# Two interleaved attention and dense layers on one core: where the last 128 output columns of a group are transposed

## The chip, the cores and the metric

The kernel runs on one core of one Trainium2 chip. The metric is the device time of one execution in microseconds (us). Before the change it is 1353.05 us, the median of 3 runs (1352.7 to 1353.13).

## The reference, cut to what matters

There are 2048 rows of width 640. A layer is a linear attention block (32 heads of 20) followed by a dense block of width 1728, each behind a layer norm and each added to its input. There are two layers with the same weights.

```python
x = x + _A_ref(_layernorm(x), A_wqkv, A_wo)      # attention block
x = x + _B_ref(_layernorm(x), B_w1, B_b1, B_w2, B_b2)   # dense block
# _B_ref: h = x @ w1 + b1;  h = max(h, 0) ** 2;  out = h @ w2 + b2
```

The change lies in the dense block, in how the last 128 of the 640 output columns get back into rows.

## The kernel before

**Tiling.** The rows are 16 tiles of 128. In the dense block a group `g` is four tiles (512 rows), so a layer has groups 0 to 3. Every matmul is done in three passes, from a high and a low part of each operand (`split`), and the sums stay in PSUM, whose eight banks of 128x512 floats have names (`FB`): `h` for fc1's result, `a0` to `a3` and `as` for fc2's sums, `po0` and `po1` for side products.

**Steps.** A group has 14 steps `c`, one for each chunk of 128 of the 1728 inner columns. In step `c`, `fc1` (L1005) makes 15 matmuls into bank `h`, transposed: inner columns on the partitions, the 512 rows of the group along the free axis. `act` applies the bias and the ReLU on ScalarE (L1017, which empties bank `h`), then squares and splits on VectorE (L1018, L1019, L1020). `fc2` (L1055) of the step before runs on TensorE behind the fc1 of this one: `pend` holds it back by one step. So TensorE's order is fc1(c), fc2(c-1), fc1(c+1), fc2(c), and fc2 of step 13 of group g runs in step 0 of group g+1.

**fc2.** It adds to five banks in the order of `i`: for `i` = 0 to 3 the bank `a<i>` holds 128 rows by output columns 0 to 511 (DM = 512). For `i` = 4 (TG) the weights and the rows change sides, and bank `as` holds output columns 512 to 639 on the partitions by all 512 rows of the group. This fifth part, the strip, is transposed and has to be turned.

**The end of a group.** In its last step fc2 does the strip first. `strip_out` (L1063) copies bank `as` to SBUF on ScalarE; TensorE goes on with `i` = 0 to 3; then `strip_turn` (L1069) does four transposes of 128x128 on TensorE into bank `po0`. On VectorE, four `tile_add`s (L1080) add the banks `a0` to `a3` to the residual rows in the tile `x1` (one buffer), and `strip_add` (L1073) adds the turned strip from `po0` to their last 128 columns. `x2_store` (L1084) then issues four stores of 128x640 on SP's queue, to the next layer's input or to the output. In the last group of the last layer `fc2_last` does the same in another order.

**What else runs beside the steps.** The attention output of the next group is made beside the steps of this one. Each step has places: `"pre"`, then 0 to 4 (after each part `i` of fc2), `"pe"` and `"post"`. A table `events`, keyed by (group, step, place), lists functions that are called there in the order in which they were entered; a place is written here as (step, place). `side` enters those of a pair of tiles. Of these, the following matter here:

- `blocks_T` (L356) and `blocks_move` (L365): a transpose without TensorE. VectorE turns each 32x32 block of a tile in place, and ScalarE then moves the blocks to their partitions with 16 copies of 32x160, four for each `j`.
- `p_split` (L1223 on ScalarE, L1225 on VectorE) and `s_turns` (L1208, L1212, L1215) prepare the operands of a pair. In groups 1 and 2, `s_turns` has its places at (8,0) to (8,3) for the second pair.
- `Pair.p1` to `p7` are the pair's products. They use the banks `po0` and `po1` in turn, in the order p1 (9,0), p4 (9,1), p6 (9,2), p7 (9,3), p5 (9,4). `p1` is read out of its bank by ScalarE (`su`, L1283), and p6 writes the same bank next; the others are added by VectorE (L1276).
- `f_bias` (L632, L633), `b_load_pq` (L573) and `b_load_x` (L577) issue stores and loads on SP.

In group 3 of layer 0, `side_last` prepares the first tiles of the next layer instead, with `blocks_move` after steps 7, 8, 9, 10, 12 and 13 and `xT_split` (L127, L128) after steps 9 and 11. Group 3 of layer 1 has no such work.

**Queues and buffers.** Every engine takes its instructions in the order written. SP issues nearly all transfers, in order: the weights come by `load_ring` (L288) into a ring of six buffers as soon as fc1 or fc2 has freed one. Working tiles of 128x640 come from one pool of twelve buffers (`ftile`). `x1_load` (L1136, at step 12) fills `x1` for the end of the group and needs the stores of the group before to be done.

Of the kernel before, what the change touches and what calls it, by code (L numbers as in the profile page):

```python
# [8 lines left out]
F32 = mybir.dt.float32  # L9
R32 = mybir.dt.float32r  # L10
AF = mybir.ActivationFunctionType
ALU = mybir.AluOpType

P = 128
# [7 lines left out]
TG = 4  # L22
GT = TG * P
B32 = 32
NG = NT // TG
# [29 lines left out]
    )  # L55

OUT0 = (3, 5, 8, 10)
TURN0 = (  # L60
# [11 lines left out]
def kernel(  # L72
# [11 lines left out]
    nc = tc.nc  # L84
# [36 lines left out]
    def ftile(name):  # L121
        return tmp.tile([P, D], F32, tag="f", name=name, bufs=F_BUFS)
# [284 lines left out]
    def rows(t, ap):  # L407
        return ap[t * P : (t + 1) * P, :]
# [23 lines left out]
    for layer in range(N_LAYERS):  # L432
# [54 lines left out]
        def rtile():  # L487
            return ap.tile([P, D], F32, tag="r", name="r", bufs=3)
# [26 lines left out]
        if layer == 0:  # L515
# [28 lines left out]
            out=mask, in_=mask, compare_op=ALU.is_ge, fill=0.0, base=0,  # L544
# [3 lines left out]
            out=mask, in_=mask, compare_op=ALU.is_ge, fill=0.0, base=DH - 1,  # L548
# [116 lines left out]
        for t in range(NT):  # L665
# [13 lines left out]
            if first:  # L679
                fk, fq = Phi(rtile()), Phi(rtile())  # L680
                for nm, f, pss in (("k", fk, (bank(0), bank(1))), ("q", fq, (bank(2), bank(7)))):
                    w = wk(nm)
                    for c in range(DC):
                        for j in range(2):
                            s = slice(j * HD, (j + 1) * HD)
# [17 lines left out]
            g = list(range(DC)) if t > 0 else []  # L703
# [9 lines left out]
            f, fq = Phi(rtile()), None if is_late else Phi(rtile())  # L713
# [248 lines left out]
        for i in (2, 3):  # L962
# [18 lines left out]
        bp = sb.enter_context(  # L981
            tc.tile_pool(name=f"b_{layer}", bufs=1, side="right", reuse_waits="tile")
        )

        def fresh(nm):
            return bank(FB[nm])
# [49 lines left out]
        accs, x1s = {}, {}  # L1036

        def fc2_tile(g, c, h, i):

            u = wu.get(g, "w2", c)  # L1040
            wh, wl = u[:, :D], u[:, D:]
            first, last = c == 0, c == NF - 1
            if first:
                accs[g, i] = fresh(f"a{i}" if i < TG else "as")
            ps = accs[g, i]
            if i < TG:
                hh, hl = (h[:, j, i * P : (i + 1) * P] for j in range(2))
                a = [(hh, wl[:, :DM]), (hl, wh[:, :DM]), (hh, wh[:, :DM])]
            else:
                hh, hl = h[:, 0], h[:, 1]  # L1050
                a = [(wl[:, DM:], hh), (wh[:, DM:], hl), (wh[:, DM:], hh)]
            if last:
                a = [a[0], a[2]]
            for k, (l, r) in enumerate(a):
                nc.tensor.matmul(  # L1055
                    ps, l, r, start=first and k == 0, stop=last and k == len(a) - 1
                )

        strips = {}

        def strip_out(g):
            strips[g] = s = bp.tile([P, GT], F32, tag="s", name="strip", bufs=1)
            nc.scalar.activation(s, accs.pop((g, TG)), AF.Copy)  # L1063

        def strip_turn(g):
            ps = fresh("po0")
            s = strips[g]
            for i in range(TG):
                nc.tensor.transpose(ps[:, i * P : (i + 1) * P], s[:, i * P : (i + 1) * P], ident)  # L1069
            strips[g] = ps  # L1070

        def strip_add(g):
            nc.vector.tensor_tensor(  # L1073
                out=x1s[g][:, :, DM:], in0=strips.pop(g)[:, :GT].rearrange("p (i n) -> p i n", i=TG),
                in1=x1s[g][:, :, DM:], op=ALU.add,
            )

        def tile_add(g, i, s=slice(0, DM)):
            v = x1s[g][:, i, s]
            nc.vector.tensor_tensor(out=v, in0=accs[g, i][:, s], in1=v, op=ALU.add)  # L1080

        def x2_store(g, i):
            t = TG * g + i
            nc.sync.dma_start(rows(t, of) if last_layer else x2[t], x1s[g][:, i])  # L1084

        def fc2(g, c, h, after=lambda i: None):
            if c < NF - 1:
                for i in range(TG + 1):
                    fc2_tile(g, c, h, i)
                    after(i)  # L1090
            else:
                fc2_tile(g, c, h, TG)
                strip_out(g)
                after(0)
                for i in range(TG):
                    fc2_tile(g, c, h, i)
                    if i < TG - 1:
                        after(i + 1)
                strip_turn(g)
                after(TG)  # L1100
                for i in range(TG):
                    tile_add(g, i)
                strip_add(g)
                for i in range(TG):
                    x2_store(g, i)
            wu.used(g, "w2", c)

        def fc2_last(g, h, hl):
# [62 lines left out]
        def m_turns(m):  # L1171

            b1 = m_whole(m)
            yield
            b2 = m_whole(m + 2)
            lo, hi = slice(0, HD), slice(HD, D)
            for i, (out, x, y) in enumerate((
                (b1[:, lo], b1[:, hi], b1[:, lo]),
                (b1[:, hi], b2[:, hi], b1[:, hi]),
                (b2[:, hi], b2[:, hi], b1[:, lo]),  # L1180
                (b2[:, lo], b2[:, lo], b2[:, hi]),
            )):
                if i % 2 == 0:
                    yield
                nc.vector.tensor_tensor(out=out, in0=x, in1=y, op=ALU.subtract)
            yield
            for u, v in ((ta, b1), (tb, b2)):
                nc.scalar.activation(u[:, 0, m], v, AF.Copy)
            for u, v in ((ta, b1), (tb, b2)):
                yield  # L1190
                nc.vector.tensor_tensor(
                    out=u[:, 1, m], in0=v, in1=u[:, 0, m].bitcast(F32), op=ALU.subtract
                )
# [134 lines left out]
        def steps(at, f, *places):  # L1328

            it = []  # L1330

            def go():
                if not it:
                    it.append(f())
                next(it[0], None)

            for p in places:
                at(*p, go)
# [44 lines left out]
        def side(g, p, plan, at):  # L1383

            t0, t1 = TG * g + 2 * p, TG * g + 2 * p + 1
            m0, m1, turn, out, back = plan["moves0"], plan["moves1"], plan["turn"], plan["out"], plan["back"]
            for t, (s, pl) in ((t0, m0), (t1, m1)):
                if t != TG:
                    at(s - 4, "post", lambda t=t: b_load_pq(t))
                den, blk = plan.get(("den", t - t0), ((s - 2, "post"), (s - 1, 1)))  # L1390
                at(*den, lambda t=t: b_den(t))
                at(*blk, lambda t=t: b_blocks(t))
                for k in range(4):
                    at(s + (pl + k) // 5, (pl + k) % 5, lambda t=t, k=k: blocks_move(yzp[t], (k,)))
            steps(at, lambda: p_split(t0), (m0[0] + 1, 0), (m0[0] + 1, 2))
            steps(at, lambda: p_split(t1, 2), (m1[0] + 1, 0), (m1[0] + 1, 1))
            steps(at, lambda: s_turns(t0), *turn)
            first = min(out.values(), key=lambda v: (v[0], v[1]))
            at(first[0] - 3, "post", lambda: b_load_x(t0))
            at(first[0] - 3, "post", lambda: b_load_x(t1))  # L1400

            def begin():
                pairs[t0] = Pair(t0)

            at(*first, begin)
            for nm, pl in out.items():
                at(*pl, lambda nm=nm: getattr(pairs[t0], nm)())

            for t, (st, ap_, (s, pl), hi, lo, bi) in ((t1, back[0]), (t0, back[1])):
                at(*st, lambda t=t: ln_stats(("b", t), xr[t]))  # L1410
                at(*ap_, lambda t=t: norm(t))
                for k in range(4):
                    at(s + (pl + k) // 5, (pl + k) % 5, lambda t=t, k=k: blocks_move(yzx[t], (k,)))
                steps(at, lambda t=t: x_split(t), hi, lo)
                at(*bi, lambda t=t: f_bias(t))


        events = {}
        for g in range(NG - 1):
            for p in range(TG // 2):  # L1420

                def at(s, place, f, g=g):
                    n = max(g * NF + s, 0)
                    events.setdefault((*divmod(n, NF), place), []).append(f)

                if g > 0:
                    side(g + 1, p, OUTS[p], at)
            if g == 0:
                for i, b in enumerate(OUT0):
                    single(i, b, OUT0[i - 1] if i else 1, at)  # L1430

                for m in range(2):
                    steps(at, lambda m=m: m_turns(m), *TURN0[m])
# [39 lines left out]
        for g in range(NG):  # L1473
            for c in range(NF):
# [10 lines left out]
                if pend:  # L1485
                    fc2(*pend, after=lambda i: run(g, c, i))
                    wu.load_ring()
                else:
                    for i in range(TG + 1):
                        run(g, c, i)  # L1490
# [46 lines left out]
```

## Time and profile before

| | us |
|---|---|
| median of 3 runs | 1353.05 |
| the profiled execution | 1352.46 |
| its span, first to last instruction | 1350.5 |
| TensorE matmul busy (6817) | 1342.5 (99%) |
| TensorE weight load busy (6817) | 1160.9 (86%) |
| VectorE busy (1625) | 912.1 (68%) |
| ScalarE busy (1931) | 770.2 (57%) |
| GpSimd busy (174) | 122.6 (9%) |

The granted TensorE clock is 1.000 over the span. The DMA queue that carries the data (q1) takes 53.8% of the time of 16 engines.

How to read the rows that follow in the prediction. A timeline row has the start and the length in us, then engine (PE is TensorE, DVE VectorE, ACT ScalarE, SPq SyncE's queue), line of the kernel, operation, output <- input, shape, and how many equal instructions were merged; a bracket gives the idle time before it and what ended it. Start times count from the first instruction. A matmul's record is longer than the time to the next one, since they are pipelined: starts are compared, not lengths. A row of the grouped view has the count, the total busy time in us, the mean of one in ns, then the idle time before.

### The profile page before, as it was taken

How to read it: one execution, taken by the hardware profiler on the slowest of the kernel's cores; microseconds unless marked ns; L12 is line 12 of the kernel's file. 1: busy time of each engine (PE TensorE's matmuls, PEld its weight loads, DVE VectorE, ACT ScalarE, POOL GpSimd, SP SyncE). 2: the span in 40 equal slices, each digit the busy share in tenths (PEclk: the TensorE clock that was granted, in tenths of full speed). 3: DMA queues.
4: the chain of work that ended last, by engine and by line, in shares of the span. 5: the costliest groups of instructions: out<-in, count | busy, mean ns of one | idle time of the engine just before them, and what ended most of it. 6: DMA issues, size and time to landing. Idle time of an engine off the chain costs nothing.

```text
span 1350.5 us, 19013 instructions
## 1 busy us (share of the span) xinstructions
PE 1342.5 (99%) x6817; PEld 1160.9 (86%) x6817; DVE 912.1 (68%) x1625; ACT 770.2 (57%) x1931; POOL 122.6 (9%) x174
## 2 busy tenths in 40 slices
PE   9999999999999999999999999999999999999998
PEld 8888998988888888888888899988888888888887
DVE  7888757777777676643467676677778667775323
ACT  5888858566546447411447688495756446464110
POOL 2222210000000000000012232100000000000000
PEclk9999999999999999999999999999999999999999
DMA  6787834574665484387521115156546646654744
GB/s 205 254 296 271 282 92 169 195 280 141 212 242 167 159 297 167 116 326 297 185 98 41 58 40 156 40 205 253 172 160 235 212 148 224 234 168 139 287 126 157
DMA packets 85635, 253.44 MB, mean 188 GB/s; under 512 B 11030, under 2 KB 19606, under 8 KB 84902
## 3 DMA queue, kind: packets, MB, share of 16 engines
q1 hardware_dynamic: 85398, 252.04, 53.8%
q8 instruction: 54, 0.88, 0.3%
q14 instruction: 39, 0.32, 0.1%
q10 hardware_dynamic: 144, 0.20, 0.0%
HBM read 193.50 MB, written 56.03 MB: 185 GB/s over the span
## 4 chain that ended last, share of the span: by engine, by line
PE 92%; DVE 4%; ACT 3%; issue 1%; POOL 0%; DMA 0%; DVEq 0%; ACTq 0%; POOLq 0%
PE PS L379 34%; PE PS L1005 28%; PE PS L1055 28%; ACT z L365 2%; PE PS L852 1%; PE PS L865 1%; DVE bn L336 0%; PE PS L521 0%; DVE kq L128 0%; DVE e L482 0%; DVE xr L621 0%; DVE r L483 0%; DVE xTb L128 0%; DMA Mr<-Mc 0%; POOL rs L341 0%
## 5 line engine op out<-in xcount | busy, mean ns | idle before, releaser
L365 ACT ACTIVATE z<-y 32x160 f32<-32x160 f32 x1424 | 475.9, 334 | 75.7 <-DVE y L356 59.4
L1005 PE MATMUL PS<-xTb,u 128*128 128x512 f32 x1400 | 333.8, 390 | 1.0 <-DVE xTb L128 1.0
L1005 PEld LDWEIGHTS PS<-xTb,u 128*128 128x128 f32 x1400 | 261.7, 188 | 54.9 <-DVE xTb L128 1.5
L379 PE MATMUL PS<-kq,xT 128*128 128x320 f32 (+2 forms) x1635 | 294.0, 334 | 1.1 <-DVE kq L128 0.6
L379 PEld LDWEIGHTS PS<-kq,xT 128*128 128x128 f32 x1635 | 259.0, 188 | 28.9 <-DVE rl L483 1.0
L1055 PE MATMUL PS<-u,h 128*128 128x512 f32 x1120 | 276.8, 390 | 0.0
L1055 PEld LDWEIGHTS PS<-u,h 128*128 128x128 f32 x1120 | 208.6, 188 | 40.8
L1017 ACT ACTIVATE hr<-PS,b1sb 128x512 f32<-128x512 f32 x104 | 71.4, 686 | 295.7 <-PE PS L1005 295.0
L1018 DVE TENSOR_TENSOR hr<-hr 128x512 f32<-128x512 f32 x104 | 71.8, 691 | 218.3 <-ACT hr L1017 217.9
L379 PE MATMUL PS<-kh,xh 128*128 128x512 f32 x480 | 124.3, 393 | 0.0
L475 ACT ACTIVATE e<-PS 128x320 f32<-128x320 f32 (+4 forms) x128 | 53.6, 435 | 102.5 <-PE PS L379 99.0
L340 POOL TENSOR_SCALAR rs<-mv 128x1 f32<-128x1 f32 x64 | 28.0, 438 | 871.1 <-DVE mv L338 871.1
L379 PE MATMUL PS<-uM,pT 128*128 128x320 f32 x648 | 102.6, 309 | 0.7 <-DVE uM L881 0.7
L379 PEld LDWEIGHTS PS<-uM,pT 128*128 128x128 f32 x648 | 97.7, 188 | 3.1 <-DVE uM L881 1.2
L379 PEld LDWEIGHTS PS<-kh,xh 128*128 128x128 f32 x480 | 87.4, 188 | 15.0
L482 DVE TENSOR_SCALAR e<-e 128x320 f32<-128x320 f32 (+4 forms) x128 | 42.6, 333 | 79.6 <-ACT e L475 79.2
L1055 PE MATMUL PS<-h,u 128*128 128x512 f32 x280 | 79.0, 390 | 0.0
L1020 DVE TENSOR_TENSOR h<-hr,h 128x512 fp32r<-128x512 f32 x104 | 72.0, 692 | 3.6
L650 POOL TENSOR_TENSOR acc<-acc,r 128x640 f32<-128x640 f32 x30 | 53.8, 1792 | 199.1 <-DVE r L483 199.1
L1055 PEld LDWEIGHTS PS<-h,u 128*128 128x128 f32 x280 | 52.2, 188 | 10.8 <-DVE h L1031 0.4
L1005 PE MATMUL PS<-xTb,uw 128*128 128x512 f32 x240 | 57.1, 389 | 0.0
L483 DVE SCALAR_TENSOR_TENSOR r<-PS,e 128x512 f32<-128x512 f32 (+2 forms) x104 | 51.1, 492 | 5.8 <-ACT e L475 2.3
(119 smaller groups left out, 1337.6 us busy)
## 6 DMA issues: line engine op xcount, KB each, us to landing
u<-kept_w SPq DMA_DIRECT2D x184, 640.0 KB, 4.7
x<-x SPq DMA_DIRECT2D x48, 320.0 KB, 5.7
kept_w<-uprep SPq DMA_DIRECT2D x23, 640.0 KB, 4.7
pqt<-pq SPq DMA_DIRECT2D x32, 320.0 KB, 4.6
x<-xr SPq DMA_DIRECT2D x32, 320.0 KB, 3.9
st<-in_B_w_dram SPq DMA_DIRECT2D x22, 320.0 KB, 5.8
pq<-r SPq DMA_DIRECT2D x20, 320.0 KB
kept_kq<-kq SPq DMA_DIRECT2D x10, 640.0 KB, 6.8
```

What stands on the lines that cost most here:

```text
L340: nc.gpsimd.tensor_scalar(rs, mv[:, 1:2], LN_EPS, None, op0=ALU.add)
L365: nc.scalar.activation(zv[j * B32 : (j + 1) * B32, :, i, :], yv[i * B32 : (i + 1) * B32, :, j, :], AF.Copy)
L379: nc.tensor.matmul(ps, a, b, start=first and i == 0, stop=last and i == 2)
L475: nc.scalar.activation(self.e[:, a:b], ps, AF.Exp)
L482: nc.vector.tensor_scalar(e, e, 1.0, PHI_EPS, op0=ALU.min, op1=ALU.add)
L483: nc.vector.scalar_tensor_tensor(out=self.r[:, a:b], in0=ps, scalar=0.0, in1=e, op0=ALU.max, op1=ALU.add)
L650: nc.gpsimd.tensor_tensor(out=acc, in0=acc, in1=r, op=ALU.add)
L1005: nc.tensor.matmul(ps, a[:, d, :], bb[:, d, :], start=d == 0 and i == 0, stop=d == DC - 1 and i == len(seq) - 1,)
L1017: nc.scalar.activation(r, ps, AF.Relu, bias=b1sb[:, c : c + 1])
L1018: nc.vector.tensor_tensor(out=r, in0=r, in1=r, op=ALU.mult)
L1020: nc.vector.tensor_tensor(out=h[:, 1], in0=r, in1=h[:, 0].bitcast(F32), op=ALU.subtract)
L1055: nc.tensor.matmul(ps, l, r, start=first and k == 0, stop=last and k == len(a) - 1)
```

## The change

In groups 0 to 2 of each layer (`beside`), the strip is no longer turned by TensorE. `strip_blocks` has VectorE turn the 32x32 blocks straight out of bank `as` into an SBUF tile, after the four `tile_add`s and in the place where `strip_add` was. `strip_moves` has ScalarE bring the blocks to their partitions with 16 copies of 32x128, four at each of the places (8,0), (8,2), (8,4) and (9,0) of the next group, into a tile `sz` from the pool of twelve. `strip_end` at (9,2) adds the result on VectorE and issues the four stores. These are entered in `events` ahead of the side work, so they come first at their places. `strip_out` and `strip_turn` remain for group 3.

```diff
+STRIP = ((8, 0), (8, 2), (8, 4), (9, 0), (9, 2))
...
+        def strip_tile():
+            return bp.tile([P, GT], F32, tag="s", name="strip", bufs=1)
+
         def strip_out(g):
-            strips[g] = s = bp.tile([P, GT], F32, tag="s", name="strip", bufs=1)
+            strips[g] = s = strip_tile()
             nc.scalar.activation(s, accs.pop((g, TG)), AF.Copy)
+
+        def strip_blocks(g):
+            y = strip_tile()
+            nc.vector.transpose(out=y, in_=accs.pop((g, TG)))
+            strips[g] = [y]
+
+        def strip_moves(g, j):
+            if j == 0:
+                strips[g].append(ftile("sz"))
+            y, z = (
+                a[:, :GT].rearrange("p (t j q) -> p t j q", t=TG, q=B32) for a in strips[g]
+            )
+            for i in range(P // B32):
+                nc.scalar.activation(
+                    z[j * B32 : (j + 1) * B32, :, i, :], y[i * B32 : (i + 1) * B32, :, j, :], AF.Copy
+                )
+
+        def strip_end(g):
+            strips[g] = strips[g][1]
+            strip_add(g)
+            for i in range(TG):
+                x2_store(g, i)
...
             else:
+                beside = g < NG - 1
                 fc2_tile(g, c, h, TG)
-                strip_out(g)
+                if not beside:
+                    strip_out(g)
                 after(0)
                 for i in range(TG):
                     fc2_tile(g, c, h, i)
                     if i < TG - 1:
                         after(i + 1)
-                strip_turn(g)
+                if not beside:
+                    strip_turn(g)
                 after(TG)
                 for i in range(TG):
                     tile_add(g, i)
-                strip_add(g)
-                for i in range(TG):
-                    x2_store(g, i)
+                if beside:
+                    strip_blocks(g)
+                else:
+                    strip_add(g)
+                    for i in range(TG):
+                        x2_store(g, i)
...
         for g in range(NG - 1):
+            for k, p in enumerate(STRIP):
+                f = (lambda g=g, k=k: strip_moves(g, k)) if k < 4 else (lambda g=g: strip_end(g))
+                events.setdefault((g + 1, *p), []).append(f)
             for p in range(TG // 2):
```

## The prediction

> **What bounds the kernel now.** I read the page first: the span, and the chain of work that ended last.
>
> ```profile
> span 1350.5 us, 19013 instructions
> ...
> PE 92%; DVE 4%; ACT 3%; issue 1%; POOL 0%; DMA 0%; DVEq 0%; ACTq 0%; POOLq 0%
> PE PS L379 34%; PE PS L1005 28%; PE PS L1055 28%; ACT z L365 2%; PE PS L852 1%; PE PS L865 1%; DVE bn L336 0%; PE PS L521 0%; DVE kq L128 0%; DVE e L482 0%; DVE xr L621 0%; DVE r L483 0%; DVE xTb L128 0%; DMA Mr<-Mc 0%; POOL rs L341 0%
> ```
>
> TensorE carries 92% of the chain, and L1005 and L1055 (fc1 and fc2 of the dense block, where the change is) carry 28% each. So in this stage a microsecond taken from TensorE is a microsecond of time, as long as no other engine becomes late. Next I read the timeline of TensorE around one turn, that at the end of group 0 in layer 0, and around a step with no turn, for comparison.
>
> ```profile
> 369.89 0.60 PE L1069 MATMUL PS<-ident,strip 128*128 128x128 f32 x4
> 370.25 3.70 PE L1005 MATMUL PS<-xTb,u 128*128 128x512 f32 x15
> 373.78 2.89 PE L1055 MATMUL PS<-u,h 128*128 128x512 f32 x12
> 376.51 0.84 PE L1055 MATMUL PS<-h,u 128*128 128x512 f32 x3
> ```
>
> ```profile
> 432.82 3.56 PE L1005 MATMUL PS<-xTb,u 128*128 128x512 f32 x15
> 436.22 0.84 PE L1055 MATMUL PS<-u,h 128*128 128x512 f32 x3
> ```
>
> The first column is the start. The four transposes begin at 369.89 and fc1 at 370.25, so they hold the array for 0.36 us, not for the 0.60 of their records, which overlap. The 15 matmuls of fc1 behind them take 373.78 - 370.25 = 3.53 us; without a turn ahead they take 436.22 - 432.82 = 3.40. So one turn costs 0.36 + 0.13 = 0.49 us. The last turn that the change touches (layer 1, group 2) has the same 3.53:
>
> ```profile
> 1256.40 3.69 PE L1005 MATMUL PS<-xTb,u 128*128 128x512 f32 x15
> 1259.93 1.29 PE L1055 MATMUL PS<-u,h 128*128 128x512 f32 x5
> ```
>
> **What the change removes.** Of the 32 transposes of the next row, 24 go: six turns of four. I call them turn 0, 1 and 2 of a layer, after the group that ends.
>
> ```profile
> L1069 PE MATMUL PS<-ident,strip 128*128 128x128 f32 x32 | 4.8, 272 | 0.0
> ```
>
> Gross saving: 6 x 0.49 = 2.94 us. (The record of one lasts 272 ns. The Trainium skill, TensorE: Matmul & The Clock Gate, Part 4: PE-mode transpose, gives about 275 ns for one in a kernel, and VectorE: DVE Perf Modes, Rules for kernel authors, says to do 128x128 transposes on TensorE where a PSUM destination is fine, which speaks against this change. The record agrees with the figure; by it the sum would be 24 x 0.275 = 6.6 us, but the starts above are 0.36 us apart for four.) The ScalarE copy L1063 goes as well; ScalarE is not on the path there, so that is worth nothing.
>
> **What then comes late.** With the turn gone, fc2 of the next step reaches bank a0 0.49 us earlier, and a0 must first have been read by the first of the four tile_adds (L1080). Timelines of VectorE at turn 0 of layer 0, and of VectorE and TensorE at the same turn of layer 1:
>
> ```profile
> 372.87 2.48 DVE L1080 TENSOR_TENSOR x<-PS,x 128x512 f32<-128x512 f32 x4
> 375.26 0.68 DVE L1073 TENSOR_TENSOR x<-PS,x 128x512 f32<-128x512 f32 x1
> ```
>
> ```profile
> 1040.03 2.48 DVE L1080 TENSOR_TENSOR x<-PS,x 128x512 f32<-128x512 f32 x4
> ```
>
> ```profile
> 1040.95 1.30 PE L1055 MATMUL PS<-u,h 128*128 128x512 f32 x5
> ```
>
> One add lasts 0.68 (the L1073 row has its shape) and they start 0.60 apart. At turn 0 the first ends at 373.55. How soon TensorE goes on after VectorE is read at the start of this stage:
>
> ```profile
> 254.15 1.55 DVE L128 TENSOR_TENSOR xTb<-PS,xTb 128x640 fp32r<-128x640 f32 x2
> ```
>
> ```profile
> 255.76 7.08 PE L1005 MATMUL PS<-xTb,u 128*128 128x512 f32 x30 [0.49 <-DVE xTb L128]
> 262.67 0.62 PE L1055 MATMUL PS<-u,h 128*128 128x512 f32 x2
> ```
>
> VectorE ends at 255.70, TensorE starts at 255.76: 0.06 us. The 30 matmuls then take 6.91, against 2 x 3.40 = 6.80: a restart costs another 0.11. So at turn 0 fc2 would like to start at 373.78 - 0.49 = 373.29, may start at 373.55 + 0.06 = 373.61, waits 0.32 and loses 0.11 more: 0.06 of the 0.49 is left. In layer 1 it wants 1040.46, gets 1040.03 + 0.68 + 0.06 = 1040.77: 0.31 + 0.11, so 0.07 is left. Nothing in the change makes these adds earlier; VectorE's work ahead of them is untouched. The later adds (0.60 apart) keep ahead of the matmuls on a1 to a3 (0.68 apart).
>
> At turn 1 (end of group 1) and turn 2 the adds are early enough:
>
> ```profile
> 481.88 2.48 DVE L1080 TENSOR_TENSOR x<-PS,x 128x512 f32<-128x512 f32 x4
> ```
>
> ```profile
> 483.27 2.88 PE L1055 MATMUL PS<-u,h 128*128 128x512 f32 x12
> 485.99 0.84 PE L1055 MATMUL PS<-h,u 128*128 128x512 f32 x3
> 486.67 0.62 PE L1005 MATMUL PS<-xTb,u 128*128 128x512 f32 x2
> ```
>
> ```profile
> 485.30 0.69 ACT L1017 ACTIVATE hr<-PS,b1sb 128x512 f32<-128x512 f32 x1
> ```
>
> ```profile
> 1256.49 2.48 DVE L1080 TENSOR_TENSOR x<-PS,x 128x512 f32<-128x512 f32 x4
> ```
>
> Turn 1: allowed at 481.88 + 0.68 + 0.06 = 482.62, wanted at 482.78. Turn 2 of layer 1: allowed at 1257.23, wanted at 1259.44. Two steps on, fc1 needs bank h, which the ReLU L1017 must have read: wanted at 486.67 - 0.49 = 486.18, allowed at 485.30 + 0.69 + 0.06 = 486.05. That spare of 0.13 is the tightest place of all; if it is missed, the loss is the shortfall plus 0.11. I take turns 1 and 2 at the full 0.49.
>
> **What the change adds.** On VectorE, strip_add (L1073, 0.68) is replaced by a block transpose of 128x512 from PSUM, which the trace doesn't show. Nearest row:
>
> ```profile
> L356 DVE STREAM_TRANSPOSE y<-pqt 128x640 f32<-128x640 f32 x32 | 27.0, 844 | 1.0
> ```
>
> It is for 640 columns; 128 fewer should save about a fifth, so I take 0.70 us, with 1.24 (the longest 128x640 row, xh<-xt L128, below) as the upper end; a shorter one gains nothing. It now also holds bank "as", which TensorE wants last of the five: at turn 0 at 373.61 + 0.11 + 2.73 = 376.45. It starts at 375.26, so it may last 1.13 before it costs anything; at turn 1 it starts at 481.88 + 4 x 0.60 = 484.28, "as" is wanted at 485.99 - 0.49 = 485.50, so 1.16. At 0.70: nothing.
>
> ```profile
> L128 DVE TENSOR_TENSOR xh<-xt,xh 128x640 fp32r<-128x640 f32 x32 | 39.5, 1235 | 0.0
> ```
>
> On ScalarE there are 16 new copies of 32x128 a turn, four each at places (8,0), (8,2), (8,4), (9,0). They are like L365, with 128 for 160 elements a partition; rows for the bounds:
>
> ```profile
> L365 ACT ACTIVATE z<-y 32x160 f32<-32x160 f32 x1424 | 475.9, 334 | 75.7 <-DVE y L356 59.4
> ```
>
> ```profile
> L1063 ACT ACTIVATE strip<-PS 128x512 f32<-128x512 f32 x8 | 4.7, 593 | 4.6 <-PE PS L1055 4.6
> ```
>
> A little below 0.334, I take 0.31, and 0.32 with the gap to the next; the far end is 0.593, and shorter ones gain nothing. Steps 8 and 9 of group 1, ScalarE, and the product p6 on TensorE:
>
> ```profile
> 429.72 0.69 ACT L1017 ACTIVATE hr<-PS,b1sb 128x512 f32<-128x512 f32 x1
> 430.30 0.52 ACT L1223 ACTIVATE pT<-z 128x384 fp32r<-128x384 f32 x1
> 434.94 1.26 ACT L1212 ACTIVATE uS<-z 128x640 fp32r<-128x640 f32 x2 [4.12 <-DVE z L1208]
> 436.42 0.69 ACT L1017 ACTIVATE hr<-PS,b1sb 128x512 f32<-128x512 f32 x1 [0.23 <-PE PS L1005]
> 437.97 0.44 ACT L1283 ACTIVATE su<-PS 128x320 f32<-128x320 f32 x1 [0.86 <-PE PS L379]
> ```
>
> ```profile
> 440.48 1.04 PE L379 MATMUL PS<-uT,uS 128*128 128x320 f32 x6
> ```
>
> The first eight copies (2.56) fit in the idle 4.12 ahead of uS. The third four follow uS: 436.20 + 1.28 = 437.48; the ReLU then takes 0.58 to the next start (430.30 - 429.72), so 438.06; the last four end at 439.34; su at 439.78. p6 (440.48) reuses the bank that su reads: spare 440.48 - 439.78 - 0.06 = 0.64. So this is hidden, at a price of nothing. In group 3 of layer 0 twelve copies (3.84) go into an idle time of 3.33 ahead of the ReLU of step 9:
>
> ```profile
> 647.36 0.69 ACT L1017 ACTIVATE hr<-PS,b1sb 128x512 f32<-128x512 f32 x1 [3.33 <-PE PS L1005]
> ```
>
> It is 0.5 late. An fc2 of 3.40 lies between it and the next fc1, and it takes 0.69, so about 2.5 was spare.
>
> strip_add comes back at (9,2) on VectorE, from SBUF (0.69, as in the next row), behind p4's add and ahead of p6's. The four stores go from step 0 to behind it on SP:
>
> ```profile
> 438.40 0.69 DVE L1020 TENSOR_TENSOR h<-hr,h 128x512 fp32r<-128x512 f32 x1
> ```
>
> ```profile
> 436.41 7.73 SPq L288 DMA_DIRECT2D u<-kept_w  x2
> ```
>
> ```profile
> 375.97 2.01 SPq L1084 DMA_DIRECT2D x<-x  x4
> ```
>
> The ReLU of step 9 starts at 437.48 in place of 436.42, 1.06 late, so L1020 ends near 440.15; with p4's add (half as wide as an add of 0.68) and itself, strip_add ends near 441.3. The four issues take 2.01, to 443.3; the next weight load is the second of the first SP row, which ends at 436.41 + 7.73 = 444.14. No load is held. In group 3 the load behind them may be 2 us late, and with six buffers in the ring and two units a step it is for a use three steps (20 us) on. The x1 tile, a single buffer, is wanted again only at step 12.
>
> **Sum.** 4 x 0.49 + 0.06 + 0.07 = 2.09 us. Against the profiled execution's 1352.46 (span 1350.5 and 2 us around it): 1350.4. That run lies 0.59 below the median of 1353.05, so the forecast for a median is **1351.0**, 0.15% faster; a measurement of this kernel can tell about 0.2% (2.7 us) from no change.
>
> **Rivals.**
> - *All six turns pay in full* (the adds are not the limit at turn 0): 1353.05 - 2.94 = 1350.1, 0.22% faster. Against it: 373.55 is the end of an add that must come first. 12%.
> - *The transposes cost their records*: 24 x 0.272 = 6.5 us, 1346.5. The starts, 0.36 apart for four, speak against it. (The Trainium skill's 275 ns, in TensorE: Matmul & The Clock Gate, Part 4, gives much the same.) 2%.
> - *The transpose out of PSUM is slow and holds bank "as"*: at 1.24 it costs 0.11 + 0.11 at the two turns 0, 0.08 + 0.11 at the two turns 1: 0.8, so 1351.8; at 1.6 it takes all of the gain: 1353.2. For it: no transpose here reads PSUM; against it: adds with a PSUM operand (0.68) are as fast as the same width in SBUF (0.69). 12%.
> - *Slower: the copies hold up su*, and TensorE waits for its bank at p6 in groups 1 and 2 of both layers. It decides from 440.48 - 0.06 - (436.20 + 0.58 + 0.44) = 3.20 for eight copies, 0.40 each. At the far end, 0.60 with its gap, each place loses 1.60 + 0.11, together 6.8: 1353.05 - 2.1 + 6.8 = 1357.8. Against it: the longer copy L365 takes 0.334. 8%.
>
> **How the numbers follow.** Forecast 66% (its own range 1350.6 to 1351.5). Faster by over 0.2%: the first two rivals, 0.14. Slower: the last, 0.08. Within 0.2%: 0.78. The range goes from 1350.0 (all turns in full) to 1353.2 (the slow transpose) and leaves out a tenth.
>
> **What would show it.** Right: TensorE waits about 0.3 us for the first tile_add at the two turns 0 and nowhere else new; fc1 behind a turn takes 3.40; the new transpose lasts about 0.70, a copy about 0.31; su ends more than 0.06 ahead of p6. Wrong: a wait of TensorE at p6, at "as", or on bank h two steps behind turn 1.

## The result, and the profile after

The changed kernel takes 1351.01 us, the median of 22 runs (1350.32 to 1351.31); the kernel before takes 1352.89 (1352.39 to 1353.82, 22 runs). The ratio is 0.9985, with a 95% interval of 0.9979 to 0.9991. The forecast was 1351.0. The gain of 1.9 us is 0.14%. The interval leaves out 1, but the gain is below the 0.2% that was set as the bound of what a measurement can tell; where it comes from is read from the traces.

The page of the changed kernel: its span, and TensorE's busy time.

```profile
span 1348.6 us, 19071 instructions
## 1 busy us (share of the span) xinstructions
PE 1340.0 (99%) x6793; PEld 1157.7 (86%) x6793; DVE 914.9 (68%) x1631; ACT 796.9 (59%) x2021; POOL 122.6 (9%) x174
```

24 matmuls fewer (6817 to 6793), 2.5 us less of TensorE. ScalarE has 90 instructions more and works 27 us longer, and TensorE does not wait for it: the new work lies beside TensorE's. Next, TensorE and VectorE at turn 0 of layer 0 (line numbers are now 2 higher in fc1 and fc2, 28 in tile_add: L1007, L1057, L1108).

```profile
368.81 1.30 PE L1057 MATMUL PS<-u,h 128*128 128x512 f32 x5
369.94 3.56 PE L1007 MATMUL PS<-xTb,u 128*128 128x512 f32 x15
373.65 3.05 PE L1057 MATMUL PS<-u,h 128*128 128x512 f32 x12 [0.15 <-DVE x L1108]
376.55 0.62 PE L1057 MATMUL PS<-h,u 128*128 128x512 f32 x2
```

```profile
372.92 2.48 DVE L1108 TENSOR_TENSOR x<-PS,x 128x512 f32<-128x512 f32 x4
375.31 0.71 DVE L1073 STREAM_TRANSPOSE strip<-PS 128x512 f32<-128x512 f32 x1
```

The transposes are gone and fc1 follows fc2 at once. But fc2 does not start at 369.94 + 3.40 = 373.34: it waits until the first tile_add (372.92 + 0.68 = 373.60) has left bank a0, and starts at 373.65. By the starts that is a wait of 0.31; the bracket has 0.15, because it counts from the end of the last record of fc1, and records are longer than the distance between starts. The part on bank "as" begins at 376.55, against 376.51 before the change, and this execution is 0.05 later since its start-up. So the turn has given 0.01, which is next to nothing. At turn 1, for comparison:

```profile
479.43 3.56 PE L1007 MATMUL PS<-xTb,u 128*128 128x512 f32 x15
482.83 2.88 PE L1057 MATMUL PS<-u,h 128*128 128x512 f32 x12
485.55 0.84 PE L1057 MATMUL PS<-h,u 128*128 128x512 f32 x3
486.23 1.98 PE L1007 MATMUL PS<-xTb,u 128*128 128x512 f32 x8
```

There fc1 takes 3.40, as without a turn, and the fc1 after it starts at 486.23 in place of 486.67; with the 0.05 of start-up that is the whole 0.49. The list of waits of TensorE has one new row (the last; the two before it are old):

```profile
PE PS L381 <- DVE uM L883: 0.7, 2, 0.4
PE PS L381 <- DVE GT L515: 0.4, 1, 0.4
PE PS L1057 <- DVE x L1108: 0.3, 2, 0.2
```

It comes twice, at the two turns 0, and counts like the bracket. What each turn gives can be read for every kernel in one way: take the start of the same matmul in the trace of before and in that of the kernel, well ahead of a turn and well behind it, and see by how much the difference changes. Start-up, which differs by up to 0.8 us from one execution to the next, drops out.

| kernel | turn 0 | turn 1 | turn 2 | turn 0 | turn 1 | turn 2 |
|---|---|---|---|---|---|---|
| (us; minus is gained) | layer 0 | | | layer 1 | | |
| the change | -0.01 | -0.49 | -0.49 | -0.01 | -0.49 | -0.49 |
| e1_adds_first | -0.20 | -0.49 | -0.49 | -0.23 | -0.49 | -0.49 |
| e2_two_groups | 0.04 | -0.49 | -0.49 | 0.04 | -0.49 | -0.49 |
| e3_turns_kept | 0.02 | 0.01 | 0.01 | 0.01 | 0.01 | 0.01 |
| e4_adds_first_moves | -0.50 | -0.49 | -0.49 | -0.50 | -0.49 | -0.49 |
| e7_before_adds_first | -0.01 | 0.00 | 0.00 | -0.01 | 0.00 | 0.00 |

The rest of the side work, steps 8 and 9 of group 1 on ScalarE, then VectorE's and SP's part of it:

```profile
434.98 1.26 ACT L1246 ACTIVATE uS<-z 128x640 fp32r<-128x640 f32 x2 [1.52 <-DVE z L1242]
436.26 1.26 ACT L1083 ACTIVATE sz<-strip 32x128 f32<-32x128 f32 x4
437.55 0.69 ACT L1019 ACTIVATE hr<-PS,b1sb 128x512 f32<-128x512 f32 x1
438.27 1.27 ACT L1083 ACTIVATE sz<-strip 32x128 f32<-32x128 f32 x4
439.56 0.44 ACT L1317 ACTIVATE su<-PS 128x320 f32<-128x320 f32 x1
```

```profile
440.55 0.68 DVE L1101 TENSOR_TENSOR x<-sz,x 128x512 f32<-128x512 f32 x1
```

```profile
441.26 2.00 SPq L1112 DMA_DIRECT2D x<-x  x4
443.86 0.32 SPq L290 DMA_DIRECT2D u<-kept_w  x1
```

```profile
440.52 1.04 PE L381 MATMUL PS<-uT,uS 128*128 128x320 f32 x6
```

su is out of its bank at 440.00 and p6 starts at 440.52, with no wait; the stores are issued by 443.26, and the weight load behind them goes out at 443.86.

### The profile page after: what moved, and what is told of

Same layout as the page of the kernel before. It is cut to its first block, busy times and chain, and to the rows that moved or that the text cites. A ratio compares the mean times of both kernels' runs of the same rounds, so it can differ in the third digit from the quotient of the medians.

```text
span 1348.6 us, 19071 instructions
## 1 busy us (share of the span) xinstructions
PE 1340.0 (99%) x6793; PEld 1157.7 (86%) x6793; DVE 914.9 (68%) x1631; ACT 796.9 (59%) x2021; POOL 122.6 (9%) x174
## 4 chain that ended last, share of the span: by engine, by line
PE 89%; DVE 5%; ACT 3%; issue 1%; DMA 1%; POOL 0%; SPq 0%; DVEq 0%; ACTq 0%
PE PS L381 34%; PE PS L1057 27%; PE PS L1007 27%; ACT z L367 2%; PE PS L854 1%; PE PS L867 1%; DMA st<-in_A_wqkv_dram 0%; DVE bn L338 0%; DVE e L484 0%; DVE xr L623 0%; DVE r L485 0%; DVE xTb L130 0%; DMA Mr<-Mc 0%; POOL rs L343 0%; DVE y L358 0%
## 5 line engine op out<-in xcount | busy, mean ns | idle before, releaser
L1007 PE MATMUL PS<-xTb,u 128*128 128x512 f32 x1400 | 333.1, 389 | 1.0 <-DVE xTb L130 1.0
L1007 PEld LDWEIGHTS PS<-xTb,u 128*128 128x128 f32 x1400 | 262.0, 188 | 55.3 <-DVE xTb L130 1.5
L1057 PE MATMUL PS<-u,h 128*128 128x512 f32 x1120 | 277.1, 390 | 0.3 <-DVE x L1108 0.3
L1057 PEld LDWEIGHTS PS<-u,h 128*128 128x128 f32 x1120 | 208.4, 188 | 41.9 <-DVE x L1108 1.2
L1057 PE MATMUL PS<-h,u 128*128 128x512 f32 x280 | 79.0, 390 | 0.0
L1057 PEld LDWEIGHTS PS<-h,u 128*128 128x128 f32 x280 | 52.1, 188 | 10.8 <-DVE h L1033 0.4
L1007 PE MATMUL PS<-xTb,uw 128*128 128x512 f32 x240 | 57.0, 389 | 0.0
```

The source lines that it names most:

```text
L1007: nc.tensor.matmul(ps, a[:, d, :], bb[:, d, :], start=d == 0 and i == 0, stop=d == DC - 1 and i == len(seq) - 1,)
L1057: nc.tensor.matmul(ps, l, r, start=first and k == 0, stop=last and k == len(a) - 1)
```

## The experiments

Theory A is the prediction's: TensorE sets the time; a turn costs it 0.49 us; at the two turns 0 the first tile_add takes the place of the turn. Rivals: B, each turn gives a third and the adds are no limit; C, the gain comes from what moved, not from the transposes; D, the side work has room to spare, and its places don't matter. E and F are named where they come up. The ratios are to the kernel before, timed beside each.

**e1_adds_first and e4_adds_first_moves: take the wait of turn 0 away.** In fc2's last step the adds and the block transpose go ahead of the places' side work; e4 also moves four of ScalarE's copies of step 0 behind the ReLU of step 1.

```diff
-                after(0)
                 for i in range(TG):
                     fc2_tile(g, c, h, i)
-                    if i < TG - 1:
-                        after(i + 1)
...
-                after(TG)
                 for i in range(TG):
                     tile_add(g, i)
                 if beside:
                     strip_blocks(g)
-                else:
+                for i in range(TG + 1):
+                    after(i)
+                if not beside:
```

```diff
-OUTS = ({**fast(2), ("den", 1): ((-1, 1), (-1, 3))}, fast(9))
+OUTS = ({**fast(2), "moves1": (0, 2), ("den", 1): ((-1, 1), (-1, 3))}, fast(9))
```

> The changed kernel (1351.0 us), with the four tile_adds and the block transpose put ahead of the side work of places 0 to 4 on VectorE in the last fc2 of a group. Theory A (TensorE sets the time; at the two turns 0 it waits for the first tile_add, which stands behind side work on VectorE): the wait of about 0.15 us and its restart go at both turns 0, and TensorE reaches bank h 0.45 us earlier two steps on. There the ReLU of step 1 ends at 376.83, 0.06 before TensorE may go on, and TensorE wants the bank at about 376.78: a new wait of about 0.1 and a restart of about 0.15. So 0.2 us a turn 0 is gained: about 1350.6 us. Rival B (each of the three turns of a layer gives the same and the adds aren't a limit): 1351.0 us, no wait changed.

Measured: 1350.58 us (0.9982, 0.9973 to 0.9991). The wait for the add is gone, and the new one for bank h is there. TensorE, then ScalarE:

```profile
376.70 0.84 PE L1057 MATMUL PS<-h,u 128*128 128x512 f32 x3
377.51 0.74 PE L1007 MATMUL PS<-xTb,u 128*128 128x512 f32 x2
```

```profile
376.77 0.69 ACT L1019 ACTIVATE hr<-PS,b1sb 128x512 f32<-128x512 f32 x1
```

Three matmuls of 0.227 end at 377.38; fc1 starts at 377.51, 0.05 after the ReLU has left bank h (377.46).

> The kernel e1_adds_first, with the moves of the second tile of the first pair in groups 1 and 2 two places later ((0,2) in place of (0,0)), so that four of the twelve copies ahead of the ReLU of step 1 go behind it and it runs about 1.4 us earlier. Theory A: the new wait for bank h that e1_adds_first should have goes as well, and both turns 0 give their full 0.48 us: 1351.0 - 2 x 0.47 = 1350.1 us. Rival B: 1351.0 us. If e1_adds_first gains and this one gains no more, bank h was not what held it.

Measured: 1350.26 us (0.9981, 0.9972 to 0.9990). ScalarE and TensorE at turn 0:

```profile
374.74 0.69 ACT L1019 ACTIVATE hr<-PS,b1sb 128x512 f32<-128x512 f32 x1
375.45 1.37 ACT L367 ACTIVATE z<-y 32x160 f32<-32x160 f32 x4
```

```profile
374.10 2.88 PE L1057 MATMUL PS<-u,h 128*128 128x512 f32 x12
376.82 0.84 PE L1057 MATMUL PS<-h,u 128*128 128x512 f32 x3
377.50 1.75 PE L1007 MATMUL PS<-xTb,u 128*128 128x512 f32 x7
```

The ReLU ends at 375.43 and TensorE runs through: 0.50 at each turn 0, as at the others. So what held turn 0 was first the add and, right behind it, bank h. B falls. The three ratios of the change, e1 and e4 overlap; that they differ is shown by the table of turns, and by e4 against e2 below (1350.26 and 1351.10 on one chip).

**e2_two_groups: leave turn 0 out of the change.**

```diff
-                beside = g < NG - 1
+                beside = 0 < g < NG - 1
...
-            for k, p in enumerate(STRIP):
+            for k, p in enumerate(STRIP if g > 0 else ()):
```

> The change in groups 1 and 2 only; group 0 of each layer turns its strip on TensorE as before the change. Theory A: turn 0 gave back nearly all of its 0.49 us, so leaving it out costs 0.02 us a layer: 1351.0 us, as with the whole change. Rival B (each turn gives a third of a layer's gain): two thirds of the 1.9 us remain, 1351.6 us.

Measured: 1351.10 us (0.9986, 0.9977 to 0.9995): as the whole change. The two theories lie 0.6 us apart, less than the interval tells; the table decides, with 0.04 at the turns 0 and -0.49 at the other four. Theory A holds.

**e3_turns_kept: put the array time back, and nothing else.** At the six turns:

```diff
                 if not beside:
                     strip_turn(g)
+                else:
+                    ps = fresh("po0")
+                    for i in range(TG):
+                        nc.tensor.transpose(ps[:, i * P : (i + 1) * P], b2bc[:, i * P : (i + 1) * P], ident)
```

> The changed kernel, with four transposes of 128x128 put back on TensorE at each of the six turns, of columns of the constant b2bc and into bank po0, where nobody reads them. All else of the change stays (no ScalarE copy at the turn, block transpose, 16 copies, stores at step 9). Theory A: the gain is the array time of the transposes alone, so all of it goes: 1352.9 us. Rival C (the gain comes from the ScalarE copy that is gone, or from the stores that have moved): 1351.0 us stays.

Measured: 1353.16 us (1.0001, 0.9992 to 1.0010). At turn 1:

```profile
479.91 0.60 PE L1134 MATMUL PS<-ident,b2bc 128*128 128x128 f32 x4
480.27 3.69 PE L1007 MATMUL PS<-xTb,u 128*128 128x512 f32 x15
483.79 2.88 PE L1057 MATMUL PS<-u,h 128*128 128x512 f32 x12
```

0.36 for the four and 3.52 for fc1, as before the change. All of the gain was array time; C falls. It also settles the rival of the full records: 24 transposes cost about 2 us here, and not 6.5. The 275 ns of the Trainium skill, TensorE: Matmul & The Clock Gate, Part 4: PE-mode transpose, would make it 6.6, an estimate; the figure agrees with a record's length (272 ns), and not with what one adds here.

**e7_before_adds_first: the same order of adds in the kernel before.** The edit is that of e1, with strip_turn kept ahead of the adds and strip_add behind the places.

> The kernel before the change, with the four tile_adds ahead of the side work of places 0 to 4 on VectorE, as in e1_adds_first, and the turn kept on TensorE. Theory A (before the change nobody waited for the adds, which were 0.17 us early at turn 0): 1352.9 us, no change. Rival E (the earlier adds are worth something by themselves, and e1_adds_first's gain has nothing to do with the turn): 1352.5 us.

Measured: 1352.95 us, against 1353.16 for the kernel before (1.0000, 0.9991 to 1.0009). Rival E asked for 1352.5, which the interval alone does not rule out; the shifts do, with -0.01 at the turns 0 and nothing at the others, although the adds of turn 0 start at 372.38 there and at 372.87 before. The order of the adds is worth nothing as long as the turn hides them; E falls.

**e6_blocks_thrice: hold bank "as" longer.**

```diff
-            nc.vector.transpose(out=y, in_=accs.pop((g, TG)))
+            ps = accs.pop((g, TG))
+            for _ in range(3):
+                nc.vector.transpose(out=y, in_=ps)
```

> The changed kernel, with the block transpose out of bank as made three times over, so that VectorE holds the bank about 1.25 us longer. Theory A (TensorE wants the bank at 376.55 at turn 0 and at 485.55 at turn 1, and gets it 0.06 after the last transpose, at 377.3 and 486.2): waits of 0.77 and 0.68 with a restart of 0.17 at two turns each, 2 x 0.94 + 2 x 0.85 = 3.6, about 1354.6 us; nothing at turn 2. Rival D (a step has room on VectorE): 1351.0 us.

Measured: 1355.68 us (1.0017, 1.0008 to 1.0027), 1.1 more than expected. TensorE and VectorE at turn 0:

```profile
374.16 3.04 PE L1057 MATMUL PS<-u,h 128*128 128x512 f32 x12
378.08 0.96 PE L1057 MATMUL PS<-h,u 128*128 128x512 f32 x3 [0.88 <-DVE strip L1075]
```

```profile
375.82 2.21 DVE L1075 STREAM_TRANSPOSE strip<-PS 128x512 f32<-128x512 f32 x3
```

The place and the mechanism are right, and by the shifts it is the turns 0 and 1 that pay: TensorE starts 0.05 after the last transpose (378.03). The size was not: three transposes into one tile follow each other at 0.75, and not overlapped at 0.62, so the bank was held 1.5 us longer. This is the rival of the slow transpose, and it exists; at 0.71 the transpose stays clear of it.

**e5_copies_twice, e8_last_four_twice, e9_six_more: more copies ahead of su.** In strip_moves, the copies are repeated: all of the third and the fourth four (e5, 8 more), those of the fourth four (e8, 4 more), two and four (e9, 6 more). For e5:

```diff
-            for i in range(P // B32):
+            for i in (*range(P // B32), *(range(P // B32) if j > 1 else ())):
```

> The changed kernel (1351.0 us), with each copy of the third and the fourth four made twice (at places (8,4) and (9,0)), so 16 copies in place of 8 stand between uS and su on ScalarE. Theory A (the copies are hidden as long as su is read out of its bank before p6; the spare is 440.52 - 440.00 = 0.52 us less 0.06, and a copy takes 0.318 with its gap): su ends 8 x 0.318 = 2.54 later, TensorE waits 2.1 us at p6 and loses 0.11 to 0.17 at the restart, in groups 1 and 2 of both layers: 4 x 2.2 = 8.9, about 1359.9 us. Rival D (ScalarE has room, its copies cost TensorE nothing): 1351.0 us.

Measured: 1364.07 us (1.0078, 1.0064 to 1.0092), 4.2 more than expected. The wait is as worked out; what follows it is not. TensorE in group 1 of layer 0 and, behind the dots, at the same place in group 1 of layer 1; then four windows of TensorE's granted clock (PEclk, third column from the right), one behind the wait of each place: groups 1 and 2 of layer 0, then of layer 1:

```profile
440.29 0.86 PE L1057 MATMUL PS<-u,h 128*128 128x512 f32 x3
443.24 1.67 PE L381 MATMUL PS<-uT,uS 128*128 128x320 f32 x6 [2.09 <-ACT su L1317]
444.70 1.48 PE L1057 MATMUL PS<-u,h 128*128 128x512 f32 x3
445.98 1.52 PE L381 MATMUL PS<-uT,uS 128*128 128x320 f32 x6
447.34 0.86 PE L1057 MATMUL PS<-h,u 128*128 128x512 f32 x3
...
1117.15 1.15 PE L381 MATMUL PS<-uT,uS 128*128 128x320 f32 x6 [2.08 <-ACT su L1317]
```

```profile
443.62:447.03 3.41, 3.41 (x13) 3.12 (x12) 0.49 (x1) 0.00 (x0) 0.00 (x0) 0.50 0.83 314
...
556.26:559.67 3.41, 3.41 (x12) 3.13 (x13) 0.58 (x2) 0.00 (x0) 0.00 (x0) 0.50 0.53 195
...
1117.15:1121.15 4.00, 4.00 (x24) 3.74 (x25) 1.91 (x4) 0.00 (x0) 0.00 (x0) 1.00 0.75 285
...
1228.68:1232.10 3.42, 3.42 (x12) 3.13 (x13) 0.52 (x2) 0.00 (x0) 0.00 (x0) 0.50 0.76 290
```

Behind three of the four waits the array runs at half its clock for 3.41 us; three 512-column matmuls take 1.28 us (444.70 to 445.98) and not 0.68. Such a place then costs 3.90 us more than in the changed kernel, and 2.35 where the clock stays (from the shifts across the place), so the clock adds about 1.5. Two more kernels take the wait apart from the clock.

> The changed kernel (1351.0 us), with only the four copies at (9,0) made twice: four more copies ahead of su, half of what e5_copies_twice has. There the wait at p6 was 2.08 us a place and the granted clock was 0.5 for 3.41 us behind three of the four waits. Theory A with the spare of 0.46: a wait of 4 x 0.318 - 0.46 = 0.81 and a restart of 0.17 at four places, 3.9 us, clock 1.0: 1354.9 us. Theory F (any wait of TensorE here drops the clock): 3.41 us at half speed cost 1.7 more at each place, 1361.7 us.

Measured: 1354.90 us (1.0014, 1.0004 to 1.0024).

> The changed kernel with six more copies ahead of su (two at (8,4), four at (9,0)), between e8_last_four_twice and e5_copies_twice. Theory A: a wait of 6 x 0.318 - 0.46 = 1.45 and 0.17 at four places, 6.5 us: 1357.5 us with the clock at 1.0. Where the clock drops behind a wait of this length, 1.7 us is added for each place, up to 1364.3 us; how many places drop is what the run is to show.

Measured: 1357.88 us (1.0037, 1.0024 to 1.0050). The first row of TensorE's waits, in e8 and in e9:

```profile
PE PS L381 <- ACT su L1317: 2.9, 4, 0.7
```

```profile
PE PS L381 <- ACT su L1317: 5.7, 4, 1.4
```

Four waits each, and the granted clock is 1.000 over both spans. By the shifts a place costs 0.99 us with four copies more, 1.69 with six and 2.35 with eight where the clock stays: from the point where the cover ends the price grows nearly evenly, by about 0.34 a copy. F falls: a wait of 1.4 did not drop the clock at any of four places, one of 2.1 did at three of four. D falls with e5, e6, e8 and e9.

## Why the prediction was right

- **The path.** TensorE carries the time and a turn costs it 0.49 us: measured 0.49 at the four turns where nothing came late, and e3 gives it back whole.
- **Turn 0.** That the first tile_add would come late there: shown by the new wait, by e1 and by e4. The wait was 373.65 - 373.34 = 0.31, as worked out. The restart behind it was sized too small: 0.11 was taken from a restart of fc1; here 12 matmuls take 2.90 us (373.65 to 376.55) and not 12 x 0.227 = 2.72, so it is 0.18. In e4, where nothing is waited for, they take 2.72 (374.10 to 376.82). Hence 0.01 was left of each turn 0, and not 0.06 or 0.07. This is the one term of the sum that was off: about 1.97 by the shifts and not 2.09, and 1.9 between the medians.
- **The last digit is luck.** The gain was put 0.2 us too high against the medians, and the forecast started from 1353.05, the median of three runs, where the 22 runs of the kernel before have 1352.89. The two errors are of nearly the same size and cancel, so 1351.0 met 1351.01.
- **Bank h two steps behind turn 1.** Called the tightest place, with 0.13 to spare; the ReLU (485.24 in the changed kernel) ends 0.30 ahead of fc1, 0.24 less the latency, so it held. What the prediction did not see is that at turn 0 the same bank is the next limit, once the adds are early (e1).

```profile
485.24 0.69 ACT L1019 ACTIVATE hr<-PS,b1sb 128x512 f32<-128x512 f32 x1
```

- **The new instructions.** The block transpose out of PSUM was put at 0.70 and a copy at 0.31; the grouped view of the changed kernel has 706 and 307 ns:

```profile
L1083 ACT ACTIVATE sz<-strip 32x128 f32<-32x128 f32 x96 | 29.5, 307 | 1.2
L1073 DVE STREAM_TRANSPOSE strip<-PS 128x512 f32<-128x512 f32 x6 | 4.2, 706 | 0.0
```

- **The cover at p6.** Put at 0.64; measured 440.52 - 440.00 - 0.06 = 0.46. The ReLU takes 0.72 to the start of the copy behind it (437.55 to 438.27), and not 0.58. At step 8 the same two instructions start 0.59 apart (429.77 to 430.35), so the kind of instruction behind the ReLU is not the reason; which it is stays open. It changed nothing, but the slower rival began at 0.38 a copy, not at 0.40. Its mechanism is real (e8, e9, e5). Its price at the far end, 1.71 us a place, was put too low: at 0.60 a copy the wait would be 8 x (0.60 - 0.38), about 1.8 us and not 1.60, and e9 paid 1.69 for a wait of 1.4 already. Whether the clock would drop behind a wait of 1.8 was not run.
- **The stores.** They were put at 441.3 to 443.3, the rows have 441.26 to 443.26.

## What to carry to other kernels

What an edit takes off the bound engine is the distance between starts with and without it, and not the records of the instructions removed. Then move everything behind it up by that much and look for the first reader of a buffer that was on time by less: at turn 0 it was an add that nobody had waited for, and behind it a ReLU. Moving those two (e4) makes the version that was fastest here, 1350.26 us.

## What the runs showed of the hardware

- A wait of TensorE of 2.1 us, amid work at full clock, was followed by 3.41 us at a granted clock of 0.50 at three places of four; waits of 1.4 us and less (12 in e6, e8 and e9) were not.
- Why three of four: the trace of e5 has the clock drop at 443.62, 556.26 and 1228.69 and come back at 447.03, 559.67 and 1232.10. From each of these six to the next in time it is 1, 32 or 196 times 3.413 us, so in this trace the clock changes on a fixed grid of 3.413. On this grid three of the waits lie whole in the stretch that ends where the clock drops (441.15 to 443.24 in 440.21 to 443.62; 554.05 to 556.13; 1226.41 to 1228.50). The fourth, 1115.06 to 1117.15, has a line of the grid at 1116.05 in it, which leaves 0.99 us idle in one stretch and 1.10 in the next. In e9 two waits of 1.43 (441.38 to 442.81 and 1110.95 to 1112.38) lie whole in a stretch, with the grid laid from the change of the clock at 1355.45, and the clock stayed. So 2.09 us of idle time out of 3.41 dropped the clock for the next stretch, and 1.43 did not; where between them it turns was not run.
- The Trainium skill, TensorE: Matmul & The Clock Gate, Part 1: The HAM clock gate, tells of a free-running window of 3413 ns; the traces agree with it (3.413 us). Its advice (same page, Why this matters for your kernels) is to avoid gaps over some 3 us, and that is too lenient for this case, where 2.09 was enough.
- The four runs of e5 took 1361.62, 1363.21, 1364.93 and 1365.09 us, with a granted clock of 0.999, 0.997, 0.996 and 0.996. A stretch of 3.41 us at 0.50 takes 0.00125 from the mean of a span of 1361 us, so this fits one, two, three and three such stretches; a time that falls apart in steps of 1.6 to 1.7 us is what they leave behind.
- A restart of TensorE costs 0.11 to 0.18 us beyond the wait (0.11 in fc1 at the start of the stage, 0.18 in fc2 at turn 0), as matmuls start further apart: at turn 0 the first two by 0.34 us and the eleven others by 0.225 to 0.236, in place of 0.227. TensorE goes on 0.05 to 0.06 us after the other engine has ended.
- Three VectorE transposes of 128x512 into one tile start 0.74 and 0.75 us apart (e6), where the four tile_adds, each into its own part of x1, start 0.60 apart.
